# A convolution and a gated network on one core: layer-norm sums on ScalarE for 13 of 16 blocks, x ahead of the weights, and a new order of steps

## The chip, the core and the metric

One core of a Trainium2 chip. The metric is device time in microseconds of one execution, the median of several runs. Names used here: TensorE (PE) multiplies matrices, VectorE (DVE) and ScalarE (ACT) work element by element, GpSimd (POOL) does small side work, SyncE (SP) issues nearly all the DMAs. Each engine runs its own queue of instructions in order; semaphores make one wait for another.

## What is computed

The reference, cut to what matters (S = 2048 tokens, D = 640, F = 1728, all tensors bfloat16):

```python
xn = layernorm(x)                                   # over D, eps 1e-5
# branch A: a short convolution, a long one, a gate
k_shift = sum(k_pad[:, t:t + S, :] * shift_k[:, 3 - t] for t in range(4))
kv = k_shift * v
y = irfft(rfft(kv, 2 * S) * rfft(ssm_k, 2 * S))[:S] + kv * ssm_D
a = xn * y
# branch B: a gated network
h = sigmoid(xn @ w_gate) * (xn @ w_up)
out = x + a + h @ w_down
```

## The kernel before

The 2048 tokens lie as 128 partitions x 16 blocks; one block is a tile of 128 x 640. Four blocks are a group g, and four groups are the four passes t of branch B.

**Norm.** For a block, `ln_stats` (L198) runs two bn_stats over halves of 320 on VectorE, `ln_aggr` (L202) makes mean and variance of them, `ln_var` adds eps, `ln_pow` takes the power -1/2 on GpSimd, and `ln_xn` (L219) writes the normalised block xn on VectorE. In group 0, TensorE transposes a block (`xn_mm`, L233) and ScalarE copies it to xnT (`xn_ev`, L236); the two together are `turn(i)`. In groups 1 to 3 a DMA transposes it (`xn_turn`, L240).

**Branch B.** The 1728 columns are 14 chunks fc of 128, the last one a half chunk. For each chunk `gate_mm` and `up_mm` (L260) make a product of 128 x 512 from five matmuls. `gate_ev` (L269) takes the sigmoid on ScalarE, `up_ev` (L275) multiplies on VectorE and writes hT. `both_mm`, `both_ev` and `both_mul` do the last half chunk. `down_mm` (L304) makes half of a token block's output in two parts of seven matmuls each, and `down_ev` (L309) adds it into x. In pass t = 0 the first two chunks are done token block by token block (`quarter`, L251: five matmuls of 128 x 128), so that they can start when the first block is normalised. gate, up, down and the last products of branch A share four PSUM buffers: a product can start when the fourth product before it has been taken away by its `gate_ev`, `up_ev` or `down_ev`.

**Branch A.** D is five chunks c of 128 channels. `kv_op` (L337 to L346) makes k_shift * v on VectorE: 8 steps for each half of the tokens, the last of which multiplies by v. `h_turn` (L323) transposes the long filter hn on VectorE, `add_D` adds ssm_D on GpSimd. The long convolution is a Fourier transform in two stages: `st1_mm` (L363, L365; eight matmuls a step), `st1_ev` (L223, tile t), a store and a load through HBM (`wr1`, `rd2`), `st2_mm` (L396), `st2_ev`, `prod` on VectorE (L409, L411), and back: `inv1_mm` (L425), `inv1_ev`, `wr2`, `rdb`, `inv2_mm` (L464), and `inv2_q`, `inv2_x`, which gate by xn and add into x. The st1, st2 and inv1 steps share two large PSUM buffers.

**Order.** Start, first group and quarters are written out. All else is put into chains, one letter for each kind of step (g for gate, up and down matmuls, s for gate_ev and both_ev, u for up_ev, both_mul and down_ev, k for kv_op, m for the first loads, and so on), and a string ORDER of 845 letters says from which chain the next step is taken. That string is the order of every engine's queue, SP's too. DMAs go round eight semaphores, so a DMA is issued when the eighth before it has landed.

Of the kernel before, what the change touches and what calls it, by code (L numbers as in the profile page):

```python
# [57 lines left out]
def kernel(  # L58
# [14 lines left out]
    nc = tc.nc  # L73
    xr = A_q.flatten_outer_dims().rearrange("(p b) d -> p b d", b=NB)
# [14 lines left out]
    cv = ctx.enter_context(tc.tile_pool(name="cv", bufs=1))  # L89
    dr = ctx.enter_context(tc.tile_pool(name="dr", bufs=1, space=bass.MemoryType.DRAM))  # L90
# [14 lines left out]
    x = res.tile([P, NB, DM], BF16, name="x")  # L105
    xn = res.tile([P, NB, DM], BF16, name="xn")
# [14 lines left out]
    sync = nc.sync  # L121
# [49 lines left out]
    def load_w(eng, lo, hi, u):  # L171
        if u == 0:
            eng.dma_start(w[:, :, lo:hi], wgr[:, :, lo:hi])  # L173
            return
        h = min(hi, 13 * P)
        eng.dma_start(w[:, :, UP + lo:UP + h], wur[:, :, lo:h])  # L176
# [9 lines left out]

    lns = [dict() for _ in range(4)]

    def ln_stats(g, i):
        b = 4 * g + i  # L190
        d = lns[g]
        if i == 0:
            d["st"] = cv.tile([P, 4, 2, nc.vector.BN_STATS_DIM], F32, name="st")
            d["mv"] = cv.tile([P, 4, nc.vector.BN_AGGR_DIM], F32, name="mv")
            d["var"] = cv.tile([P, 4], F32, name="var")
            d["rstd"] = cv.tile([P, 4], F32, name="rstd")
        for s2 in range(2):
            nc.vector.bn_stats(d["st"][:, i, s2, :], x[:, b, s2 * 320:(s2 + 1) * 320])  # L198

    def ln_aggr(g, i):  # L200
        d = lns[g]
        nc.vector.bn_aggr(d["mv"][:, i, :], d["st"][:, i, :, :])  # L202

    def ln_norms(g, i):
        ln_stats(g, i)
        ln_aggr(g, i)

    def ln_var(g, lo, hi):
        d = lns[g]
        nc.vector.tensor_scalar(d["var"][:, lo:hi], d["mv"][:, lo:hi, 1], 1e-5, None, op0=ALU.add)  # L210

    def ln_pow(g, lo, hi):
        d = lns[g]
        nc.gpsimd.tensor_tensor(d["rstd"][:, lo:hi], d["var"][:, lo:hi], mhalf[:, lo:hi], ALU.pow)

    def ln_xn(g, i):
        b = 4 * g + i
        d = lns[g]
        nc.vector.tensor_scalar(xn[:, b, :], x[:, b, :], d["mv"][:, i, 0:1], d["rstd"][:, i:i + 1],  # L219
                                op0=ALU.subtract, op1=ALU.mult)  # L220
# [9 lines left out]
    def xn_mm(i):  # L230
        xts[i] = pt = psC.tile([P, NC, P], BF16, name="pt", tag="c")
        for c in range(NC):
            nc.tensor.transpose(pt[:, c, :], xn[:, i, c * P:(c + 1) * P], ident[:])  # L233

    def xn_ev(i):
        nc.scalar.copy(out=xnT[:, i, :, :], in_=xts[i][:, :, :])  # L236
# [8 lines left out]
    def quarter(u, fc, i):  # L245

        if i == 0:
            pgs[u, fc] = psG.tile([P, 512], F32, name=("pg", "pu")[u], tag="g")
        o = u * UP + fc * P
        for c in range(NC):  # L250
            nc.tensor.matmul(pgs[u, fc][:, i * P:(i + 1) * P], lhsT=w[:, c, o:o + P], rhs=xnT[:, i, c, :],  # L251
                             start=(c == 0), stop=(c == NC - 1))
# [3 lines left out]
    def product(u, fc):  # L256

        pg = psG.tile([P, 512], F32, name=("pg", "pu")[u], tag="g")
        for c in range(NC):
            nc.tensor.matmul(pg[:, :], lhsT=w[:, c, u * UP + fc * P:u * UP + (fc + 1) * P], rhs=xnT[:, :, c, :],  # L260
                             start=(c == 0), stop=(c == NC - 1))
# [93 lines left out]
    def st1_mm(c, n):  # L355

        h, n4 = divmod(n, 4)
        if n == 0:
            chunks[c]["d1"] = dr.tile([P, 2, NB, 2 * P], BF16, name="d1", bufs=2)
        pss[n] = ps = psC.tile([P, 4, 2 * P], F32, name="ps1", tag="c")  # L360
        for i in range(4):
            b = 4 * n4 + i
            nc.tensor.matmul(ps[:, i, 0:P], lhsT=S1[:, b, h, :], rhs=cin[c]["kvh"][:, 0, b, :], start=True, stop=True)  # L363
            hp = cin[c]["kvh"][:, 1, :, :].rearrange("p b c -> p (b c)").rearrange("p (b c e) -> p b e c", b=8, e=2)
            nc.tensor.matmul(ps[:, i, P:2 * P], lhsT=S1[:, b, h, :], rhs=hp[:, b // 2, b % 2, :], start=True, stop=True)  # L365
# [111 lines left out]
    for b in range(2):  # L477
        for i in range(2):
            (sync, nc.scalar)[i].dma_start(x[:, b, 320 * i:320 * i + 320], xr[:, b, 320 * i:320 * i + 320])
    for u in range(2):  # L480
        load_w((sync, nc.scalar)[u], 0, P, u)
    for i in range(2):
        (sync, nc.scalar)[i].dma_start(x[:, 2 + i, :], xr[:, 2 + i, :])
# [92 lines left out]
    for c in range(NC):  # L576
# [54 lines left out]
    step("o", store, NB - 1, NB, 4 * P, DM)  # L631

    ORDER = """
    mmmmmmmmmggggsmmsumggsguuZsgggmukksmgmskmukgkggkmuksHgsggumkuggskgukHgskgmkmuggmkTsksgKuugkDagaAgkmA
    uaHKtHmwmagllllAglgDPkAuaAwmklllahuelgekAugekakkugaggAgkggkAakaukuewgkukmkkgsTggAkuwsngkVutAgaskwkgs
    AKgaukgrHkaAgAualakswkgAagVguskrAgAbgkwTksuBkBskkguKDgskkHlkaagguAlAKkngbtwushungpkplBsBgaAwgaugkpKl
    gksaupgAAPlglswkVslrgkuKaueaglHAwaggkkAAVDcwCggTkaCkukuaAgregHkkAbggkugBBKkuurpbBgeklgBkgpbpgBluBpeg
    atawAkuWggskuaklpghuAwasgAAgaarluAkHrkggAcVskgkJupgsCbgDswBugkBuspaAaKklgPgpAbugBkFsWrgRkcVCCsgugpdH
    rsbpBkgBugWqudbsgplkpgrBBcurgqRCsqJgbgWkwgukgswpBrBlubksBFqgusludapdqaglgeAaguggRqAeaquAwAappgAaepqe
    ggIcgCuwguJbBgpFdgrbpqugWBuqdpqBrgcugJpqgrCbugpsRwBFggpbupgBdsrqBuWpgdqrcJspggqgCbuFRqBggsubpdsWugBB  # L640
    gdprscCqgpJrqgbsuBgqFRgupsgbspudpgqrWBgBduqqRcpgJCqWgsqbsBugBgpugsRdpgpucsgqJqCWdgqgusqgudgqouggudRq
    gqugoRogggqudguodqgqqdudoggqqqqgogqoouuoooooo
    """
# [35 lines left out]
```

## Time and profile before

| | |
|---|---|
| time, median of 3 runs | 238.88 us (238.79 to 239.32) |
| span of the profiled execution | 236.5 us |
| TensorE busy (PE) | 228.3 us, 97% |
| VectorE busy (DVE) | 205.5 us, 87% |
| ScalarE busy (ACT) | 120.5 us, 51% |
| GpSimd busy (POOL) | 12.7 us, 5% |
| DMA | 56.79 MB, mean 240 GB/s |

The profile is of one execution, and its rows count from its first instruction. For that execution only the span is given: it runs from the first to the last instruction, and the time of a run is 2.4 us longer at the median (238.88 against 236.5). A matmul's end in the profile is modelled, so a row's duration is longer than the step from one matmul to the next; the steps are read from the starts. The granted TensorE clock was 1.000 throughout.

How to read its rows: in the timeline, start and duration in us, engine, line, operation, out<-in, shape, and in brackets how long the engine idled before and what ended that. In the groups: total busy us, mean ns of one, then idle time before them with what ended it. In the waits: who waited for whom, us in total, times, the longest. "SPq" and "ACTq" are the issuing of DMAs.

### The profile page before, as it was taken

How to read it: one execution, taken by the hardware profiler on the slowest of the kernel's cores; microseconds unless marked ns; L12 is line 12 of the kernel's file. 1: busy time of each engine (PE TensorE's matmuls, PEld its weight loads, DVE VectorE, ACT ScalarE, POOL GpSimd, SP SyncE). 2: the span in 40 equal slices, each digit the busy share in tenths (PEclk: the TensorE clock that was granted, in tenths of full speed). 3: DMA queues.
4: the chain of work that ended last, by engine and by line, in shares of the span. 5: the costliest groups of instructions: out<-in, count | busy, mean ns of one | idle time of the engine just before them, and what ended most of it. 6: DMA issues, size and time to landing. Idle time of an engine off the chain costs nothing.

```text
span 236.5 us, 5439 instructions
## 1 busy us (share of the span) xinstructions
PE 228.3 (97%) x2200; PEld 131.2 (55%) x2201; DVE 205.5 (87%) x365; ACT 120.5 (51%) x151; POOL 12.7 (5%) x24
## 2 busy tenths in 40 slices
PE   7799979999999999999999999999999999999994
PEld 2664434877555445766663544487655444446772
DVE  5533879999999999999999999889999979998563
ACT  2342323463376787666767777663346465552000
POOL 5210000020000002000001300000000000000000
PEclk9999999999999999999999999999999999999999
DMA  6999999999999999999889888998799976575774
GB/s 175 272 267 273 238 250 314 247 293 193 232 312 306 285 278 311 250 284 210 230 244 270 215 197 221 308 264 248 180 294 254 240 200 205 148 179 136 201 232 148
DMA packets 98927, 56.79 MB, mean 240 GB/s; under 512 B 58518, under 2 KB 93142, under 8 KB 98646
## 3 DMA queue, kind: packets, MB, share of 16 engines
q1 hardware_dynamic: 97814, 55.95, 91.0%
q10 hardware_dynamic: 1088, 0.49, 0.8%
q8 instruction: 17, 0.28, 0.5%
q14 instruction: 8, 0.07, 0.1%
HBM read 36.12 MB, written 18.35 MB: 230 GB/s over the span
## 4 chain that ended last, share of the span: by engine, by line
PE 68%; DMA 11%; SPq 11%; DVE 5%; ACT 2%; issue 2%; ACTq 0%; DVEq 0%
PE pd L304 20%; PE pu L260 16%; PE pg L260 16%; DMA sraw<-in_A_shift_k_dram 5%; PE psb L464 4%; PE ps L396 3%; PE psa L425 3%; PE ps L363 3%; PE ps L365 3%; DMA hn<-in_A_ssm_k_dram 2%; DMA d<-t 2%; DMA w<-in_B_w_gate_dram 2%; SPq L176 2%; SPq L173 2%; SPq L139 2%
## 5 line engine op out<-in xcount | busy, mean ns | idle before, releaser
L260 PEld LDWEIGHTS <-w 128*128 128x128 bf16 x500 | 46.5, 98 | 56.7 <-issue 7.0
L304 PE MATMUL pd<-wd,hT 128*128 128x320 bf16 (+2 forms) x447 | 65.9, 299 | 0.1
L260 PE MATMUL pu<-xnT,w 128*128 128x512 bf16 x250 | 62.3, 380 | 1.3 <-DVE hT L275 1.3
L260 PE MATMUL pg<-xnT,w 128*128 128x512 bf16 x250 | 62.2, 379 | 0.0
L304 PEld LDWEIGHTS <-hT 128*128 128x128 bf16 x448 | 41.8, 98 | 18.4 <-issue 2.3
L269 ACT ACTIVATE sig<-pg 128x512 bf16<-128x512 f32 x52 | 30.9, 600 | 38.2 <-PE pg L260 31.2
L223 ACT CAST t<-ps 128x1024 bf16<-128x1024 f32 x39 | 38.4, 1014 | 16.7 <-PE ps L365 10.4
L275 DVE TENSOR_TENSOR hT<-sig,pu 128x512 bf16<-128x512 bf16 x52 | 35.2, 679 | 8.9 <-PE pu L260 5.6
L223 ACT CAST xz<-ps 128x1024 bf16<-128x1024 f32 x34 | 33.2, 1015 | 16.1 <-PE ps L396 14.9
L411 DVE TENSOR_TENSOR xz<-xz 128x2048 bf16<-128x2048 bf16 x20 | 24.3, 1217 | 0.1
L363 PE MATMUL ps<-kvh,S1t 128*128 128x128 bf16 x160 | 21.3, 218 | 0.3 <-ACT t L223 0.3
L365 PE MATMUL ps<-kvh,S1t 128*128 128x128 bf16 x160 | 21.3, 220 | 0.0
L341 DVE TENSOR_TENSOR tmp<-kx,sc 128x1024 bf16<-128x1024 bf16 x30 | 20.7, 689 | 0.3
L343 DVE TENSOR_TENSOR acc<-acc,tmp 128x1024 bf16<-128x1024 bf16 x30 | 20.5, 685 | 0.3
L309 DVE TENSOR_TENSOR x<-pd,x 128x320 bf16<-128x320 f32 (+2 forms) x32 | 15.4, 485 | 5.1 <-PE pd L304 4.9
L365 PEld LDWEIGHTS <-S1t 128*128 128x128 bf16 x160 | 15.4, 96 | 2.4 <-issue 0.4
L363 PEld LDWEIGHTS <-S1t 128*128 128x128 bf16 x160 | 15.5, 97 | 2.1
L198 DVE BATCH_NORM_STATS2 st<-x 128x6 f32<-128x320 bf16 x32 | 13.9, 476 | 3.1 <-DMA x<-in_A_q_dram 3.1
L469 DVE TENSOR_TENSOR yx<-psb,xn 128x512 bf16<-128x512 f32 x20 | 13.8, 688 | 2.1 <-PE psb L464 1.7
L409 DVE STREAM_SHUFFLE xz<-xz 128x512 f32<-128x512 f32 x20 | 14.5, 725 | 0.0
L223 ACT CAST ao<-psa 128x1024 bf16<-128x1024 f32 x10 | 9.9, 1013 | 8.4 <-PE psa L425 8.3
L323 DVE STREAM_TRANSPOSE kvh<-hn 128x512 f32<-128x512 f32 x10 | 10.9, 1099 | 1.5 <-DMA hn<-in_A_ssm_k_dram 1.5
(48 smaller groups left out, 150.1 us busy)
## 6 DMA issues: line engine op xcount, KB each, us to landing
d<-t SPq DMA_DIRECT2D x20, 512.0 KB, 5.0
t<-d SPq DMA_DIRECT2D x20, 512.0 KB, 4.7
bi<-d SPq DMA_DIRECT2D x8, 512.0 KB, 5.6
d<-ao SPq DMA_DIRECT2D x6, 512.0 KB, 4.6
kx<-in_A_k_dram SPq DMA_DIRECT2D x10, 256.0 KB, 5.1
hn<-in_A_ssm_k_dram SPq DMA_DIRECT2D x20, 128.0 KB, 4.0
kvh<-in_A_v_dram SPq DMA_DIRECT2D x10, 256.0 KB, 5.3
x<-in_A_q_dram SPq DMA_DIRECT2D x3, 640.0 KB, 5.3
```

The source lines that it names most:

```text
L223: nc.scalar.copy(out=out, in_=in_)
L260: nc.tensor.matmul(pg[:, :], lhsT=w[:, c, u * UP + fc * P:u * UP + (fc + 1) * P], rhs=xnT[:, :, c, :], start=(c == 0), stop=(c == NC - 1))
L269: nc.scalar.activation(sig[fc][:, :], pgs[0, fc][:, :], ACT.Sigmoid)
L275: nc.vector.tensor_tensor(hT[:, fc, :], sig[fc][:, :], pgs[1, fc][:, :], ALU.mult)
L304: nc.tensor.matmul(pd[:, :], lhsT=hT[:, fc, bb * P:(bb + 1) * P], rhs=wd[:, fc, es], start=(fc == 0), stop=(fc == NFC - 1))
L309: nc.vector.tensor_tensor(x[:, 4 * t + bb, es], pds[bb, half][:, :], x[:, 4 * t + bb, es], ALU.add)
L341: nc.vector.tensor_tensor(d["tmp"][:, :, :], kx[:, lo + 3 - m:hi + 3 - m, :], sb(m), ALU.mult)
L343: nc.vector.tensor_tensor(d["acc"][:, :, :], d["acc"][:, :, :], d["tmp"][:, :, :], ALU.add)
L363: nc.tensor.matmul(ps[:, i, 0:P], lhsT=S1[:, b, h, :], rhs=cin[c]["kvh"][:, 0, b, :], start=True, stop=True)
L365: nc.tensor.matmul(ps[:, i, P:2 * P], lhsT=S1[:, b, h, :], rhs=hp[:, b // 2, b % 2, :], start=True, stop=True)
L409: nc.vector.stream_shuffle(z[:, 2, :, :].bitcast(F32), z[:, 1, :, :].bitcast(F32), swap)
L411: nc.vector.tensor_tensor(z[:, 1:3, :, :], z[:, 0:1, :, :].to_broadcast((P, 2, 8, P)), z[:, 1:3, :, :], ALU.mult)
```

## The change

- **Norm sums.** Block 2, and all blocks of groups 1 to 3, no longer use bn_stats. Two passes of ScalarE over the block take their place (`ln_sums`): a Copy scaled by -1/640 whose running sum is minus the mean, and a Square with that as bias whose running sum is the sum of squared differences. Both write their elementwise output into xn, which is overwritten later. Variance and power are made on GpSimd for the groups (`ln_sums_pow`), on VectorE and GpSimd for block 2. VectorE normalises with an add and a multiply (`ln_sums_xn`). Blocks 0, 1 and 3 keep bn_stats.
- **First loads.** x blocks 2 and 3 are asked for before the first gate and up weights, not behind them. ScalarE's queue then issues its halves of x blocks 0 and 1, x block 3 and the first up block.
- **Start.** The first transpose stands ahead of block 3's statistics; the other three `turn`s are put between the quarters by the list FIRST.
- **HBM tiles.** d1 and d2 get a buffer for each chunk in place of two.
- **Order.** ORDER is a new string of 842 letters, and TURNS permutes the chain of the first loads (m) and that of the stores (o). In the first loads, the up weights of chunks 4 and 5 and of 8 and 9 now come ahead of the gate weights of 4 and 5; x group 1 is asked for seventh from there on, both halves of w_down late, and v's first half of chunk 1 last but for one table. VectorE evicts 19 of the large PSUM tiles, not 15.

The diff, cut:

```diff
+FIRST = """
+g00 t1 u00 t2 g10 u10 t3 g01 u01 g11 u11 g02 u02 g12 u12 g03 u03 g13 u13
+"""
...
+    def ln_sums(g, i):
+        b = 4 * g + i
+        d = ln_tile(g)
+        nc.scalar.activation(xn[:, b, :], x[:, b, :], ACT.Copy, scale=-1.0 / DM, accum_out=d["nm"][:, i:i + 1])
+        nc.scalar.activation(xn[:, b, :], x[:, b, :], ACT.Square, bias=d["nm"][:, i:i + 1],
+                             accum_out=d["ss"][:, i:i + 1])
+
+    def ln_sums_var(g, i):
+        d = lns[g]
+        nc.vector.tensor_scalar(d["var"][:, i:i + 1], d["ss"][:, i:i + 1], 1.0 / DM, 1e-5, op0=ALU.mult, op1=ALU.add)
+
+    def ln_sums_pow(g, lo, hi):
+        d = lns[g]
+        nc.gpsimd.tensor_scalar(d["var"][:, lo:hi], d["ss"][:, lo:hi], 1.0 / DM, 1e-5, op0=ALU.mult, op1=ALU.add)
+        ln_pow(g, lo, hi)
+
+    def ln_sums_xn(g, i):
+        b = 4 * g + i
+        d = lns[g]
+        nc.vector.tensor_scalar(xn[:, b, :], x[:, b, :], d["nm"][:, i:i + 1], d["rstd"][:, i:i + 1],
+                                op0=ALU.add, op1=ALU.mult)
...
-            chunks[c]["d1"] = dr.tile([P, 2, NB, 2 * P], BF16, name="d1", bufs=2)
+            chunks[c]["d1"] = dr.tile([P, 2, NB, 2 * P], BF16, name="d1", bufs=NC)
...
+    for i in range(2):
+        (sync, nc.scalar)[i].dma_start(x[:, 2 + i, :], xr[:, 2 + i, :])
     for u in range(2):
         load_w((sync, nc.scalar)[u], 0, P, u)
-    for i in range(2):
-        (sync, nc.scalar)[i].dma_start(x[:, 2 + i, :], xr[:, 2 + i, :])
...
     busy(10)
-    for i in range(4):
-        ln_stats(0, i)
-        if i:
-            ln_xn(0, i - 1)
-        ln_aggr(0, i)
-        ln_var(0, i, i + 1)
-        ln_pow(0, i, i + 1)
+    ln_stats(0, 0)
+    ln_ready(0, 0)
+    ln_sums(0, 2)
+    ln_stats(0, 1)
+    ln_xn(0, 0)
+    ln_ready(0, 1)
+    turn(0)
+    ln_stats(0, 3)
+    ln_sums_var(0, 2)
+    ln_pow(0, 2, 3)
+    ln_xn(0, 1)
+    ln_ready(0, 3)
+    ln_sums_xn(0, 2)
     ln_xn(0, 3)
-    turn(0)
     busy(3)
-    for i in range(4):
-        for k in range(4):
-            quarter(k % 2, k // 2, i)
-            if k == (0, 1, 1, 3)[i] and i < 3:
-                turn(i + 1)
+    for k in FIRST.split():
+        if k[0] == "t":
+            turn(int(k[1]))
+        else:
+            quarter("gu".index(k[0]), int(k[1]), int(k[2]))
...
-            step("l", ln_norms, g, i)
-        step("l", ln_var, g, 0, 4)
-        step("P", ln_pow, g, 0, 4)
+            step("L", ln_sums, g, i)
+        step("P", ln_sums_pow, g, 0, 4)
...
-    mmmmmmmmmggggsmmsumggsguuZsgggmukksmgmskmukgkggkmuksHgsggumkuggskgukHgskgmkmuggmkTsksgKuugkDagaAgkmA
...
+    mmgmmgsummggggsmsugmmgmgLsuuLsZgLkkggskkmggmmuusggnkLsmuLugsPmkmgumgHgggsLusguggllsuggguHggummgggkmL
...
+    TURNS = {"m": [1, 7, 4, 9, 21, 0, 20, 2, 10, 5, 6, 13, 12, 14, 8, 17, 15, 11, 22, 18, 16, 19, 23, 25, 24, 3],
+        "o": [2, 0, 4, 1, 5, 3, 7, 6, 8, 11, 10, 9, 12, 13]}
+    left = {k: iter([v[i] for i in TURNS.get(k, range(len(v)))]) for k, v in chains.items()}
```

More of the change, by code (lines that the diff above doesn't have):

```diff
@@ L187, with ln_tile @@
     lns = [dict() for _ in range(4)]
+    def ln_tile(g):
+        if "q" not in lns[g]:
+            q = cv.tile([P, 4, 4], F32, name="lnq", bufs=2)
+            lns[g] = dict(q=q, nm=q[:, 0, :], ss=q[:, 1, :], var=q[:, 2, :], rstd=q[:, 3, :])
+        return lns[g]
     def ln_stats(g, i):
         b = 4 * g + i
-        d = lns[g]
+        d = ln_tile(g)
         if i == 0:
@@ L194, in ln_stats @@
             d["mv"] = cv.tile([P, 4, nc.vector.BN_AGGR_DIM], F32, name="mv")
-            d["var"] = cv.tile([P, 4], F32, name="var")
-            d["rstd"] = cv.tile([P, 4], F32, name="rstd")
         for s2 in range(2):
@@ L202, in ln_aggr @@
         nc.vector.bn_aggr(d["mv"][:, i, :], d["st"][:, i, :, :])
-    def ln_norms(g, i):
-        ln_stats(g, i)
-        ln_aggr(g, i)
+    def ln_sums(g, i):
+        b = 4 * g + i
+        d = ln_tile(g)
+        nc.scalar.activation(xn[:, b, :], x[:, b, :], ACT.Copy, scale=-1.0 / DM, accum_out=d["nm"][:, i:i + 1])
[13 more added lines that the diff above has]
+                                op0=ALU.add, op1=ALU.mult)
     def ln_var(g, lo, hi):
@@ L418, in inv1_mm @@
         if y2 == 0:
-            d["d2"] = dr.tile([32, P, P], BF16, name="d2", bufs=2)
+            d["d2"] = dr.tile([32, P, P], BF16, name="d2", bufs=NC)
         d["pa", y] = ps = [psC.tile([P, 2, 512], F32, name="psa", tag="c") for _ in range(2)]
@@ L498, in turn, with ln_ready @@
         xn_ev(i)
+    def ln_ready(g, i):
+        ln_aggr(g, i)
+        ln_var(g, i, i + 1)
+        ln_pow(g, i, i + 1)
     busy(10)
-    for i in range(4):
-        ln_stats(0, i)
-        if i:
-            ln_xn(0, i - 1)
-        ln_aggr(0, i)
-        ln_var(0, i, i + 1)
-        ln_pow(0, i, i + 1)
+    ln_stats(0, 0)
[11 more added lines that the diff above has]
+    ln_sums_xn(0, 2)
     ln_xn(0, 3)
-    turn(0)
     busy(3)
-    for i in range(4):
-        for k in range(4):
-            quarter(k % 2, k // 2, i)
-            if k == (0, 1, 1, 3)[i] and i < 3:
-                turn(i + 1)
+    for k in FIRST.split():
[3 more added lines that the diff above has]
+            quarter("gu".index(k[0]), int(k[1]), int(k[2]))
     for fc in range(2):
@@ L519 @@
         up_ev(0, fc)
-    chains = {k: [] for k in "ABCDHKPRTVWZabcdeghklmnopqrstuw"}
+    chains = {k: [] for k in "ABCDHKLPRTVWZabcdeghklmnopqrstuw"}
     def step(k, fn, *args):
@@ L615 @@
         for i in range(4):
-            step("l", ln_norms, g, i)
-        step("l", ln_var, g, 0, 4)
-        step("P", ln_pow, g, 0, 4)
+            step("L", ln_sums, g, i)
+        step("P", ln_sums_pow, g, 0, 4)
         for i in range(4):
-            step("l", ln_xn, g, i)
+            step("l", ln_sums_xn, g, i)
         for i in range(4):
@@ L633 @@
     ORDER = """
-    mmmmmmmmmggggsmmsumggsguuZsgggmukksmgmskmukgkggkmuksHgsggumkuggskgukHgskgmkmuggmkTsksgKuugkDagaAgkmA
[L635 to L642, printed above, removed]
-    """
-    left = {k: iter(v) for k, v in chains.items()}
+    mmgmmgsummggggsmsugmmgmgLsuuLsZgLkkggskkmggmmuusggnkLsmuLugsPmkmgumgHgggsLusguggllsuggguHggummgggkmL
+    mLlmDkaaTkkkluAgkkkueAeekggggktkkekkuaaHgukAmAgsawAakgAPgsuuHlmkuKgmkkkTagskkKwwauAAggDkkgKaashtukkk
+    AkAggkgwmwsuslauaAAHgklgkkuVVskaaAAggaksgkkkwAaAggrbuugkkkwsuBBgpkKrHpDasATaAtkugsKnguwwbKBgKFgasgAa
+    AggasuskkpkkVkahwAnrLAwLgguugkpHHgaaAkAgggDcukCJLggeealuALuaIwggbrkeBBgggeurkkkVTuukkKkubggBBgbBgBpw
+    rgppkasupaAIuggstkkkukVwkWaAaAhskgugPaAarkpggAcksJCggbwsuuHHKggDBWlpgBrassupukakggpAAsbBBgggkucwkRss
+    VkkCJggbBupupdqggrrqBspWsbupgguBdBcskrJCgqgbggkFRBusubgFllpBwgaAudaggaAWdarrqqgpAAlgwpppeauqRagAIuqq
+    egeecJCuuggubFpBpWpggbrrggBBuudqdcCJwwgqpgsRWgqpbFBpggsuurbBBprpggssugucdJCWdgpbsgqFBgubBBpqsgpgspuc
+    rCgJgspqqubgugqRdBBdrbWpqqgpgsugqqBBpcCJprsuggbsuBBRdqWpgsdRRpgggsqqucuJCgggWsqduqqdqggudquqdRRooggg
+    gqoggoooqqududugqqqguqooddqqqqgggougoouooo
+    """
+    TURNS = {"m": [1, 7, 4, 9, 21, 0, 20, 2, 10, 5, 6, 13, 12, 14, 8, 17, 15, 11, 22, 18, 16, 19, 23, 25, 24, 3],
+        "o": [2, 0, 4, 1, 5, 3, 7, 6, 8, 11, 10, 9, 12, 13]}
+    left = {k: iter([v[i] for i in TURNS.get(k, range(len(v)))]) for k, v in chains.items()}
     for k in "".join(ORDER.split()):
```

## The prediction

> **What bounds the kernel now.** I read the page first, then a table of windows, then TensorE's timeline where it is not full.
>
> ```profile
> span 236.5 us, 5439 instructions
> ...
> PE 228.3 (97%) x2200; PEld 131.2 (55%) x2201; DVE 205.5 (87%) x365; ACT 120.5 (51%) x151; POOL 12.7 (5%) x24
> ...
> GB/s 175 272 267 273 238 250 314 247 293 193 232 312 306 285 278 311 250 284 210 230 244 270 215 197 221 308 264 248 180 294 254 240 200 205 148 179 136 201 232 148
> ```
> ```profile
> 45.00:135.00 90.00, 89.75 (x837) 54.24 (x835) 88.48 (x167) 59.89 (x74) 6.91 (x7) 1.00 1.02 261
> ```
>
> The columns of a window are its length, then PE, weight loads, DVE, ACT and POOL busy. From 45 to 135 us TensorE is busy for 89.75 of 90 us and VectorE for 88.48; ScalarE has a third of that stretch free. TensorE sets the end: it does the same matrix work in both kernels, so a change of order can win only what TensorE waits, and can lose as much as it is made to wait anew. VectorE is just in time for it. What TensorE waits for lies mostly before 35 us:
>
> ```profile
> 8.64 0.44 PE L251 MATMUL pu<-xnT,w 128*128 128x128 bf16 x5
> 8.92 0.44 PE L251 MATMUL pg<-xnT,w 128*128 128x128 bf16 x5
> ...
> 11.36 0.44 PE L251 MATMUL pg<-xnT,w 128*128 128x128 bf16 x5 [0.22 <-ACT xnT L236]
> ...
> 14.26 1.02 PE L260 MATMUL pg<-xnT,w 128*128 128x512 bf16 x4
> ```
> ```profile
> 31.52 1.24 PE L260 MATMUL pg<-xnT,w 128*128 128x512 bf16 x5
> 32.30 1.10 DVE L323 STREAM_TRANSPOSE kvh<-hn 128x512 f32<-128x512 f32 x1 [1.54 <-DMA hn<-in_A_ssm_k_dram]
> ...
> 34.02 1.24 PE L260 MATMUL pu<-xnT,w 128*128 128x512 bf16 x5 [1.25 <-DVE hT L275]
> ```
> ```profile
> 73.81 0.06 PE ps L365
> 73.87 1.08 PE pg L260 x5
> ...
> 226.20 0.95 PE pd L304 x7
> ...
> 233.28 0.29 DVE x L309
> ```
> ```profile
> PE ps L363 <- ACT t L223: 0.3, 1, 0.3
> ```
>
> A product of five matmuls takes 1.08 us, seven down matmuls 0.95, an st1 step of eight matmuls 0.45 (8 x 0.056). But from 31.52 to 34.02 one took 2.50: VectorE stood at h_turn, which waited for hn, with the up_ev that frees TensorE's buffer queued behind it. That is 1.4 us lost. The eviction of t costs 0.3 us more. After that I find no wait of TensorE to the end.
>
> **The change, part by part.**
>
> *Start.* The quarters (0.28 us each, 8.64 to 8.92) end at 14.26, with holes where a transpose or its copy is late. The new list puts the transposes t1 to t3 between the first quarters, and blocks 2 and 3 of x are asked for before any weight. What it cannot move is the last of the first weights:
>
> ```profile
> 3.17 0.52 SPq L176 DMA_DIRECT2D w<-in_B_w_up_dram  x1
> 3.20 0.38 ACTq L483 DMA_DIRECT2D x<-in_A_q_dram  x1
> ```
> ```profile
> w<-in_B_w_up_dram SPq DMA_DIRECT2D x1, 160.0 KB, 5.7
> x<-in_A_q_dram ACTq DMA_DIRECT2D x1, 160.0 KB, 5.0
> ```
>
> The second up block lands at 3.17 + 5.7 = 8.87, the last x block at 3.20 + 5.0 = 8.20. The bytes asked for up to that up block are the same set in both kernels, so I keep 8.87 for it. In the new list u10 needs it; behind it stand t3 and twelve quarters: 8.87 + 14 x 0.28 = 12.8, the lower bound for the first full product (14.26 now). The upper bound: the first up block is now issued by ScalarE in the place of the last x block (3.20), and if it comes no earlier than 8.87, then u00, t2 and g10 (0.84) also stand behind it, and with another 0.2 for a copy that is late (the 0.22 at 11.36) it is 13.9. I take 13.05, nearer the lower end, since the row for that place in the queue gives 8.20. Gain 1.2 (0.4 to 1.5). Block 2's sums on ScalarE stand ahead of the copy of xnT block 0; what that takes (half a us or more) is covered by the wait for the weights.
>
> *The h_turn stall.* Now the v and k loads and hn are asked for in another order, and the first h_turn stands behind the up_ev of product 10, not 7. Its hn is 7.5 MB into the loads, as before (32.3), while VectorE comes to it at 13.05 + 19.44 + 0.9 = 33.4 (18 products of 1.08 at its up product's end). The 1.4 us go, with 1.1 us to spare.
>
> *A clock for the loads.* A slice of the GB/s row is 5.91 us, so by 29.6 us the DMA engines had moved 7.24 MB and by 32.3, when hn landed, 7.9 MB: a load lands some 1.5 us after the engines have moved as much as was asked for up to and with it. By that, the gate block for product 4 (3.47 MB in the new order) lands at 16.4 and is wanted at 13.05 + 4 x 1.08 = 17.4; block group 1 of x (4.13 MB) lands at 18.9, wanted by ScalarE after gate_ev 4 at 13.05 + 5.4 + 0.85 = 19.3.
>
> *The sums.* Of the 13 blocks 12 leave VectorE in the steady stage:
>
> ```profile
> L198 DVE BATCH_NORM_STATS2 st<-x 128x6 f32<-128x320 bf16 x32 | 13.9, 476 | 3.1 <-DMA x<-in_A_q_dram 3.1
> L202 DVE BATCH_NORM_AGGREGATE mv<-st 128x2 f32<-128x12 f32 x16 | 3.3, 208 | 0.4
> L236 ACT COPY xnT<-pt 128x640 bf16<-128x640 bf16 x4 | 2.8, 692 | 7.7 <-PE pt L233 7.7
> L269 ACT ACTIVATE sig<-pg 128x512 bf16<-128x512 f32 x52 | 30.9, 600 | 38.2 <-PE pg L260 31.2 <-DVE hT L275 5.3 <-PE pg L251 0.5
> L223 ACT CAST t<-ps 128x1024 bf16<-128x1024 f32 x39 | 38.4, 1014 | 16.7 <-PE ps L365 10.4 <-DMA d<-t 5.7 <-ACT ao L223 0.5
> ```
>
> VectorE loses 12 x (2 x 0.476 + 0.208) = 13.9 us, and takes back four evictions of some 1.2 us that the new order sends to it (19 for 15). ScalarE gains 13 x 2 passes over 640 elements. No row has a pass with a running sum; between the 512-wide 0.600 and the 1024-wide 1.014, and nearest to the 0.692 copy of 640, I take 0.72 each, so 18.7 us on an engine with 116 us free. Bounds 15.6 and 26.4: neither fills it. Behind a pair of passes (1.45) stand the gate_ev of the next product; a gate_ev has 3.24 us (three products) until its buffer is wanted and takes 0.6, so one pair ahead of it is hidden, even at 2.03; it isn't where the pair also waits for x. For block group 1 of x there is 0.4 us before that begins (18.9 against 19.3), and some 2 us more before TensorE feels it.
>
> The Trainium skill, "ScalarE: Activation LUTs", Rules for kernel authors, speaks against this move: add and multiply belong on VectorE, which is faster per element. The rows agree (1.16 against 1.45 a block), but the time goes to an engine with room. By the page's figures under "What ACT_TABLE_LOAD costs" a pair would be 1.53 us, an estimate; the sum stays.
>
> *VectorE's chain.* This is where the new order is tightest. It idles longer before 40 us, since kv_op's second half waits for loads moved back. From the first down_ev (behind 23 products and three down parts: 27.7 us after the first product) up to the up_ev that up product 8 of t=1 needs, it has, by the new order, 37 kv_op, 8 down_ev, 7 up_ev, 5 normalisations and 4 h_turn. Back to back they cost:
>
> ```profile
> 34.57 0.60 DVE hT L275
> ...
> 36.36 0.60 DVE tmp L341
> 36.97 1.03 DVE kvh L323
> ...
> 55.77 0.70 DVE acc L343
> ```
>
> 37 x 0.65 + 7 x 0.60 + 4 x 1.03 + 8 x 0.40 + 5 x 0.36 = 37.4 us (0.40 and 0.36 are estimates, from the 0.60 of an up_ev by their smaller tiles), against 17 x 1.08 + 13 x 0.95 + 16 x 0.45 = 37.9 of TensorE's work in between. It has no slack there: each late input in that stretch is a wait of TensorE, one for one. Behind it VectorE runs ahead, by the 13.9 us. I allow 1.0 us of new waits there and at the t buffers (0 to 2.5), and put against it the 0.3 of the old t wait, whose surroundings are rearranged.
>
> *The rest.* d1 and d2 with a buffer per chunk remove waits of writes for old reads, which TensorE doesn't show: nothing. All shapes keep their times; the tail (last down matmul, down_ev at 233.28, one store) is the same work in the same order: some 3 us to the span's end.
>
> **Sum.** The span was 236.5 and the median 238.88: 2.4 us lie around the span, and I keep them. 238.88 - 1.2 - 1.4 - 0.3 + 1.0 = 237.0.
>
> **The rivals.**
> 1. *No new wait.* The chain's 0.5 us hold and the loads come on time: 238.88 - 2.9 = 236.0, or 235.7 with the start at its lower bound. For it: VectorE's 88.48 of 90 us shows that so close a fit held for long.
> 2. *Slower: one load pins the chain.* kv_op 7 of chunk 1 multiplies by the first half of v, which the new order asks for last of its chunk, behind four transposes, a store of t and a halo in SP's queue:
>
> ```profile
> 53.08 5.64 SPq L240 DMA_TRANSPOSE xnT<-xn  x4
> ```
> ```profile
> kvh<-in_A_v_dram SPq DMA_DIRECT2D x10, 256.0 KB, 5.3
> ```
>
> VectorE wants it after 17 kv_op, 8 down_ev, 3 h_turn, 3 normalisations and an up_ev of the chain (19.0 us): 13.05 + 27.9 + 19.0 = 60.0. By the clock of the loads (14.5 MB) it lands at 58.7. By SP's queue it can be later: the last transpose waits for a normalisation that VectorE ends 5.8 us into the chain, at 46.8; with 5.6 us of transposes and some five issues of 0.5 us behind that, v is asked for at 55 and lands at 60.3. From 60.0 on every us is TensorE's. Slower than before needs it past 62.9; landing at 64.5 gives 236.0 + 4.5 = 240.5. For it: two estimates of the landing stand on both sides of the need. Against: it must be 4 us later than the later one.
> 3. *The order hides nothing:* the waits that go come back as waits of the same size (t buffers; the gate block for product 4, 1 us ahead of its need): 2.9 us of them give 238.9.
>
> **How the numbers follow.** The forecast has 0.56, the first rival 0.16, the third 0.08, the second 0.20. About 0.2% (0.5 us) is what a measurement of this kernel can tell from no change. So faster 0.72, same 0.08, slower 0.20. The forecast's bounds are 237.0 - 0.3 - 1.0 = 235.7 and 237.0 + 0.8 + 1.5 = 239.3; the range, 235.5 to 239.3, also holds the first and the third rival, and leaves out the second.
>
> **What the profile after would show.** First full product at 13.05 (12.8 to 13.9); no gap before an up product near 33; sums of 0.65 to 0.85 us a pass and ScalarE at 58 to 60%; VectorE's busy time down by 8 to 10 us; a wait of TensorE for VectorE, if any, between 54 and 80 us. Wrong would be: a first product later than 14; TensorE waiting over 2 us between 45 and 85; a ScalarE pass over 1.1 us; a wait for weights of product 4.

## The result, and the profile after

| | before | after |
|---|---|---|
| time, median | 238.83 us (4 runs, 238.68 to 239.32) | 236.32 us (4 runs, 235.69 to 237.14) |
| profiled execution: time, span | not given, 236.5 us | 236.47 us, 234.5 us |

The ratio is 0.9901 (95% interval 0.9875 to 0.9927), a gain of 2.5 us. The forecast was 237.0 (235.5 to 239.3), with 0.72 for faster. The total is right; the runs below show that one of its three gains is not there, and that another brings nothing by itself. The ratios, here and below, leave out executions that are over 1.5% above the fastest of their kernel; the medians keep them.

The page of after, for the engines:

```profile
span 234.5 us, 5457 instructions
...
PE 227.0 (97%) x2201; PEld 130.8 (56%) x2201; DVE 198.5 (85%) x327; ACT 136.3 (58%) x199; POOL 12.1 (5%) x27
```

VectorE lost 7.0 us and ScalarE gained 15.8. The windows of after, cut at its first full product (columns: length, then PE, weight loads, DVE, ACT and POOL busy, granted clock, DMA share, GB/s):

```profile
0.00:13.87 13.87, 10.27 (x113) 7.18 (x114) 5.57 (x19) 6.44 (x12) 4.80 (x15) 1.00 0.97 226
13.87:45.00 31.13, 31.13 (x165) 15.78 (x163) 18.19 (x29) 20.23 (x45) 3.47 (x6) 1.00 1.05 284
45.00:135.00 90.00, 89.95 (x825) 54.18 (x824) 86.47 (x138) 63.40 (x87) 3.87 (x6) 1.00 0.94 250
135.00:210.00 75.00, 74.43 (x889) 38.89 (x888) 72.19 (x115) 44.41 (x55) 0.00 (x0) 1.00 0.88 231
```

From 13.87 to 135 TensorE is idle for 0.05 us: the wait at 32 is gone, and so is the one for the eviction of t. What remains stands in the waits of TensorE and in its timeline at 192 (the first three waits lie ahead of the first full product; `idle` is the tile of the multiplies whose result is not used):

```profile
PE pg L279 <- ACT xnT L264: 1.7, 1, 1.7
PE idle L522 <- DVE hT L120: 1.2, 1, 1.2
PE pt L261 <- DVE xn L247: 0.7, 1, 0.7
PE psa L453 <- DVE xz L437: 0.6, 1, 0.6
```
```profile
13.87 1.24 PE L288 MATMUL pg<-xnT,w 128*128 128x512 bf16 x5
...
191.99 0.65 PE L453 MATMUL psa<-xz,SMt 32*32 32x512 bf16 x32 [0.57 <-DVE xz L437]
```

A useful split is at the first full product. From there to the start of the last matmul there are 218.77 us in the trace of before (14.26 to 233.03) and 217.13 in that of after (13.87 to 231.00). So of the 2.0 us between the two spans 1.64 come from the steady stage and 0.39 from the start; some 3.5 us from the last matmul to the span's end are the same in both. The other 0.5 us of the measured gain lie between one profiled execution and the medians.

The steady stage repeats: the profiled execution of every later run of the new order without an edit in that stage, on three chips, took 217.12 to 217.19 us. The start does not repeat, as the experiments show.

### The profile page after: what moved, and what is told of

It is laid out like the page before. It is cut to its first block, busy times and chain, and to the rows that moved or that the text cites. A ratio compares the mean times of both kernels' runs of the same rounds, so it can differ in the third digit from the quotient of the medians.

```text
span 234.5 us, 5457 instructions
## 1 busy us (share of the span) xinstructions
PE 227.0 (97%) x2201; PEld 130.8 (56%) x2201; DVE 198.5 (85%) x327; ACT 136.3 (58%) x199; POOL 12.1 (5%) x27
## 5 line engine op out<-in xcount | busy, mean ns | idle before, releaser
L332 PE MATMUL pd<-wd,hT 128*128 128x320 bf16 (+2 forms) x448 | 64.5, 299 | 0.0
L303 DVE TENSOR_TENSOR hT<-sig,pu 128x512 bf16<-128x512 bf16 x52 | 34.7, 680 | 15.2 <-PE pu L288 11.1
L251 ACT CAST t<-ps 128x1024 bf16<-128x1024 f32 x37 | 36.0, 1013 | 18.7 <-PE ps L393 16.0
L393 PE MATMUL ps<-kvh,S1t 128*128 128x128 bf16 x160 | 20.8, 219 | 0.0
L391 PE MATMUL ps<-kvh,S1t 128*128 128x128 bf16 x160 | 20.8, 218 | 0.0
L337 DVE TENSOR_TENSOR x<-pd,x 128x320 bf16<-128x320 f32 (+2 forms) x32 | 14.9, 481 | 5.3 <-PE pd L332 5.2
L251 ACT CAST ao<-psa 128x1024 bf16<-128x1024 f32 x8 | 8.1, 1012 | 8.9 <-PE psa L453 8.8
L215 ACT ACTIVATE xn<-x 128x640 bf16<-128x640 bf16 x13 | 9.5, 732 | 3.5 <-DMA x<-in_A_q_dram 3.5
L254 DVE CAST ao<-psa 128x1024 bf16<-128x1024 f32 x8 | 9.8, 1222 | 2.0 <-PE psa L453 1.9
```

The costliest lines, as they stand in the source:

```text
L251: nc.scalar.copy(out=out, in_=in_)
L303: nc.vector.tensor_tensor(hT[:, fc, :], sig[fc][:, :], pgs[1, fc][:, :], ALU.mult)
L332: nc.tensor.matmul(pd[:, :], lhsT=hT[:, fc, bb * P:(bb + 1) * P], rhs=wd[:, fc, es], start=(fc == 0), stop=(fc == NFC - 1))
L337: nc.vector.tensor_tensor(x[:, 4 * t + bb, es], pds[bb, half][:, :], x[:, 4 * t + bb, es], ALU.add)
```

## The experiments

A run is compared with runs of before on the same chip. "Steady" is the trace's time from the first full product to the start of the last matmul.

| run | median us | before, us | ratio (95%) | first full product | steady |
|---|---|---|---|---|---|
| old start, new order | 236.72 | 238.10 | 0.9938 (0.9912 to 0.9965) | 13.26 | 217.12 |
| new start, old order | 238.08 | 238.10 | 1.0010 (0.9985 to 1.0036) | 15.26 | 218.72 |
| sums alone | 251.46 | 238.10 | 1.0580 (1.0547 to 1.0613) | 13.65 | 232.55 |
| h_turn later alone | 239.15 | 238.10 | 1.0027 (0.9997 to 1.0057) | 13.24 | 220.67 |
| after again | 236.18 | 237.57 | 0.9962 (0.9936 to 0.9988) | 13.57 | 217.13 |
| bn_stats, new order | 240.02 | 237.57 | 1.0104 (1.0078 to 1.0130) | 15.27 | 221.23 |
| VectorE + 3 us | 239.29 | 237.57 | 1.0075 (1.0052 to 1.0098) | 13.51 | 220.47 |
| start, both edits | 236.00 | 237.57 | 0.9932 (0.9906 to 0.9959) | 13.18 | 217.19 |
| block 2 on VectorE | 236.50 | 238.37 | 0.9929 (0.9900 to 0.9959) | 13.64 | 217.12 |
| new list alone | 237.08 | 238.37 | 0.9953 (0.9926 to 0.9981) | 13.96 | 217.12 |
| two buffers | 236.18 | 238.37 | 0.9919 (0.9889 to 0.9949) | 13.39 | 217.13 |
| both edits and the swap | 235.51 | 238.37 | 0.9897 (0.9865 to 0.9929) | 13.02 | 216.50 |

Each has one profiled execution, so the last two columns are of one execution each, and those of "new start, old order" and "bn_stats, new order" are of executions in which TensorE's clock fell at the start (run 2). Before spread from 236.2 to 240.5 us in 66 executions, after from 235.7 to 238.2 in 16.

**1. The new order with the old start.** The loads, the statistics of block 2 and the quarters of before, all else as in after:

```diff
+    for u in range(2):
+        load_w((sync, nc.scalar)[u], 0, P, u)
     for i in range(2):
         (sync, nc.scalar)[i].dma_start(x[:, 2 + i, :], xr[:, 2 + i, :])
-    for u in range(2):
-        load_w((sync, nc.scalar)[u], 0, P, u)
...
-    ln_sums(0, 2)
...
-    for k in FIRST.split():
+    for i in range(4):
+        for k in range(4):
+            quarter(k % 2, k // 2, i)
```

> The changed kernel with the start of before (weights ahead of x blocks 2 and 3, bn_stats for block 2, the old order of the quarters) and the new order of all later steps. Theory A: the later steps bring most of the gain, since the first full product came only 0.39 us earlier with the new start (13.87 against 14.26): 236.3 + 0.4 = 236.7 us (236.4 to 237.0), first full product at 14.2 to 14.3, no wait near 33 us. Rival B, the sizes of the prediction: the start is worth 1.2 us, so 237.5 us.

236.72 us, as theory A has it; but the first full product came at 13.26, a microsecond before the 14.26 of before with the same start. The profiled execution of before had a late load. VectorE's statistics of block 2, in before and in run 4, which has the same start:

```profile
7.06 0.89 DVE L198 BATCH_NORM_STATS2 st<-x 128x6 f32<-128x320 bf16 x2 [1.24 <-DMA x<-in_A_q_dram]
```
```profile
6.01 0.89 DVE L198 BATCH_NORM_STATS2 st<-x 128x6 f32<-128x320 bf16 x2
```

The bracket is the tell: 1.24 us idle for x in the one, none in the other, and the statistics come 1.05 us later. The 14.26 that the prediction started from was one execution's bad luck with a load.

**2. The new start with the old order.** The reverse edit.

> The kernel before with the start of the changed one alone. Theory A: the first full product comes at 13.87, 0.39 us earlier, but the h_turn in the old order still waits for hn, which lands by the bytes ahead of it at 32.3 as before, so the end moves by 0 to 0.4 us: 238.5 to 238.85 us, and the wait of TensorE near 32 us grows. Rival B, the sizes of the prediction added up: 1.2 us, 237.6 us.

No gain, as theory A says, though not by its way: TensorE has no wait near 32 in this trace, but one of 1.27 us at 72.5. The trace, of an execution of 239.26 us, shows something else. Windows of this run, from the gap ahead of the first quarter on (the eighth column is the granted clock):

```profile
5.00:8.38 3.38, 1.42 (x10) 0.58 (x9) 2.31 (x9) 2.33 (x5) 1.01 (x3) 0.99 1.26 254
8.38:11.90 3.52, 3.52 (x36) 3.52 (x36) 1.08 (x4) 1.38 (x2) 0.85 (x2) 0.53 1.18 288
11.90:15.26 3.36, 3.36 (x64) 3.36 (x62) 0.02 (x1) 1.34 (x3) 0.63 (x1) 1.00 1.03 260
```
```profile
8.38 0.69 PE L284 MATMUL pg<-xnT,w 128*128 128x128 bf16 x5 [1.66 <-ACT xnT L269]
8.87 0.74 PE L266 MATMUL pt<-ident,xn 128*128 128x128 bf16 x5
```

TensorE stood for 1.66 us, since ScalarE's pair of passes on block 2 is ahead of the copy of xnT block 0, and over the next 3.5 us its granted clock was 0.53 in the mean: a quarter took 0.53 us in place of 0.28, and the first full product came at 15.26. Of 59 runs of kernels with that pair in the first group, 8 had a mean clock of 0.984 to 0.993; in after again (run 5) the two such executions took 238.0 and 238.2 us, the other ten 235.8 to 236.8. Of 111 runs of kernels without it, before among them, none was below 0.997. Run 3 is left out of that count: its waits are longer, and all six of its executions are at 0.985 to 0.993.

**3. The sums alone.** In the order of before, ScalarE's sums in the places of bn_stats:

```diff
-            step("l", ln_norms, g, i)
-        step("l", ln_var, g, 0, 4)
-        step("P", ln_pow, g, 0, 4)
+            step("l", ln_sums, g, i)
+        step("P", ln_sums_pow, g, 0, 4)
         for i in range(4):
-            step("l", ln_xn, g, i)
+            step("l", ln_sums_xn, g, i)
```

> The kernel before, order and start unchanged, with the norm sums of groups 1 to 3 on ScalarE in the places where bn_stats stood. Theory A: TensorE did not wait for VectorE in the steady stage of before, so 13.9 us taken from VectorE bring nothing by themselves: 238.5 to 239.2 us, VectorE busy down by 13 us. Rival B: the closely filled VectorE costs TensorE time that its records do not show as waits; then a gain of over 1 us, below 237.8. Rival C: ScalarE's pair of passes stands where gate_ev or t evictions are wanted, or where x is late: over 239.5 us with new waits of TensorE for ScalarE.

Rival C, and far beyond its size: 13.4 us slower. ScalarE's timeline and TensorE's:

```profile
46.47 0.74 ACT L216 ACTIVATE xn<-x 128x640 bf16<-128x640 bf16 x1
47.11 0.20 ACT L216 ACTIVATION_READ_ACCUMULATOR xn<-x 128x1 f32 x1
47.34 0.83 ACT L217 ACTIVATE xn<-x,lnq 128x640 bf16<-128x640 bf16 x1
48.08 0.19 ACT L217 ACTIVATION_READ_ACCUMULATOR xn<-x,lnq 128x1 f32 x1
...
53.19 1.90 ACT L255 CAST t<-ps 128x1024 bf16<-128x1024 f32 x2
```
```profile
54.23 0.22 PE L395 MATMUL ps<-kvh,S1t 128*128 128x128 bf16 x1 [4.55 <-ACT t L255]
```

The old order has a group's four blocks in a row, because on VectorE that did no harm. On ScalarE they are 6.7 us (46.47 to 53.19) ahead of the evictions of t, and TensorE waits for 4.55 us of them; later groups do the same in smaller pieces, 10.7 us of waits for ScalarE in all behind the first full product. Behind the 4.55 us the granted clock is 0.50 from 54.50 to 57.80; that costs another 1.7 us, an estimate from half of these 3.3 us. So not all of the 13.4 us is the price of the sums' place. ScalarE has room, but not for four pairs in a row. After has them one by one, mostly 2.2 to 4.4 us apart (19.96, 22.12, 24.28, 28.59, and so on), and once two in a row (39.51 and 41.19).

**4. The first h_turn later.** One letter of the order of before moved behind two up_ev:

```diff
-...kukmuksHgsggumkuggskgukHgskg...
+...kukmuksgsggumkuggskgukHHgskg...
```

> The kernel before with one step moved: the first h_turn stands just ahead of the second one in the order, so two up_ev that free TensorE's buffers are no longer queued behind its wait for hn. Theory A: the 1.4 us of TensorE's wait at 31.5 to 34.0 go: 237.4 us (237.1 to 237.7), no product over 1.3 us long near 33. Rival B: VectorE, busy for 88.48 of 90 us from 45 to 135, has no slack to catch up, and the wait comes back behind it: 238.5 to 238.9 us.

Rival B: no gain, and whether the 239.15 us, a little over its range, are a loss the interval does not tell. The wait near 32 is gone and the steady stage is 1.9 us longer. The waits of TensorE in this run:

```profile
PE pg L260 <- DMA xnT<-xn: 1.0, 1, 1.0
PE ps L363 <- ACT t L223: 0.6, 1, 0.6
PE pd L304 <- issue: 0.5, 1, 0.5
```

In starts of matmuls these are 1.2 us at 59 for the first product of the next pass, 0.8 at 73 (0.4 in before) and 0.9 at 41 for a down matmul whose hT VectorE wrote late. VectorE had not gained what TensorE had: with h_turn moved it stands at the next step that needs a load, the multiply by v.

```profile
32.06 0.69 DVE L346 TENSOR_TENSOR kvh<-acc,kvh 128x1024 bf16<-128x1024 bf16 x1 [1.93 <-DMA kvh<-in_A_v_dram]
```

The largest wait is no late input of VectorE, which had normalised the first block of group 1 by 51.8 and the last by 53.3: the group's transposes stand in SP's queue behind the next chunk's hn loads. In this run, and in after:

```profile
50.41 2.98 SPq L139 DMA_DIRECT2D hn<-in_A_ssm_k_dram  x4
53.51 5.26 SPq L240 DMA_TRANSPOSE xnT<-xn  x4
```
```profile
45.62 5.27 SPq L268 DMA_TRANSPOSE xnT<-xn  x4
```

From the first full product that is 40.3 us here, 38.8 in before (53.08) and 31.8 in after. This run started a microsecond sooner than the trace of before and had a stall less, and the transposes were asked for no earlier. The first product of the next pass, in before and here:

```profile
60.24 1.24 PE L260 MATMUL pg<-xnT,w 128*128 128x512 bf16 x5
```
```profile
60.26 1.24 PE L260 MATMUL pg<-xnT,w 128*128 128x512 bf16 x5 [1.04 <-DMA xnT<-xn]
```

In before it has no wait; here TensorE is ready a microsecond sooner and waits for the transposes until the same moment. In run 2 the product starts at 59.99. So in three traces of the old order it comes within 0.3 us, whether the first full product came at 13.24, 14.26 or 15.26: the transposes, behind the loads in SP's queue, take back both the earlier start and the missing stall. Of the 1.9 us by which the steady stage is longer, 1.0 is thus only this run's earlier start. In after the last transpose landed at 54.04 and that product started at 55.72: 1.7 us to spare.

**5. After, again**, beside the next three.

> The changed kernel itself beside the others of this set. Theory A (the change is worth 2.5 us wherever it runs): 0.9901 of before. Theory B (part of it is the start, which differs from run to run with the arrival of the first loads and the granted clock): the same kernels scatter by about 1 us, the ratio is 0.990 to 0.996, and the kernel with the old start (236.72 us, 0.9938) is level with it.

Theory B. On this chip before is faster (237.57) and after the same (236.18). The old start with the new order is level with it by the ratio (0.9938). By the medians the change is worth 1.4 us here and 2.5 us in the first set; its copy with two buffers (run 11) has 2.2 us on a third chip.

**6. bn_stats on VectorE in the new order.**

```diff
-            step("L", ln_sums, g, i)
-        step("P", ln_sums_pow, g, 0, 4)
+            step("L", ln_norms, g, i)
+        step("P", ln_norms_pow, g, 0, 4)
         for i in range(4):
-            step("l", ln_sums_xn, g, i)
+            step("l", ln_xn, g, i)
```

> The changed kernel, its order unchanged, with bn_stats on VectorE again for the blocks of groups 1 to 3, each in the place where ScalarE's sums stand (block 2 of the first group stays on ScalarE). VectorE gets 12 x 1.16 = 13.9 us back, 9.3 of it between 20 and 42 us and 4.6 between 95 and 107. Theory A (VectorE is just in time, as its 37.4 us of work against 37.9 of TensorE's says): it enters that stretch late and TensorE waits, 1 to 4 us more than the changed kernel. Rival B: the 12.9 us that VectorE idles between 13.87 and 45.00 take the first eight blocks, and the last four are made up: no more than 0.5 us.

Theory A: 3.8 us more than after in the median, 4.1 in the steady stage. The windows show where:

```profile
15.27:45.00 29.73, 29.73 (x155) 14.81 (x153) 22.36 (x46) 7.67 (x13) 2.45 (x3) 1.00 1.04 282
45.00:135.00 90.00, 87.07 (x799) 52.19 (x797) 88.02 (x152) 52.55 (x65) 3.84 (x5) 1.00 0.92 235
135.00:210.00 75.00, 74.43 (x876) 39.08 (x874) 72.82 (x116) 45.97 (x57) 0.42 (x1) 1.00 0.91 239
```

VectorE still idles for 7 us before 45, yet TensorE loses 2.9 us between 45 and 135. So the sums on ScalarE are worth about 4 us in the new order and cost 13 in the old one. And the gain needs both: the new order without the sums of groups 1 to 3 is 1.0% slower than before, these sums without the new order 5.8%.

**7. Three microseconds more for VectorE.**

```diff
         else:
+            if c == 1 and lo == 0:
+                for _ in range(5):
+                    nc.vector.tensor_tensor(d["tmp"][:, :, :], d["acc"][:, :, :], d["acc"][:, :, :], ALU.mult)
             kv = d["kvh"][:, 0, lo:hi, :]
```

> The changed kernel with five more multiplies of 128x1024 on VectorE (0.6 us each, 3.0 us together; their result is not used) just ahead of the step that multiplies by the first half of v for chunk 1, at 61.05 us. Theory A (no slack in VectorE's chain): the end moves by 3.0 us less the lead that VectorE has over TensorE near 80 us, 1 to 2 us: 1 to 2 us more, TensorE waiting for VectorE between 62 and 100. Rival B: all 3.0 us come through. Rival C: VectorE makes it up and nothing comes through.

```profile
60.69 3.59 DVE L375 TENSOR_TENSOR tmp<-acc 128x1024 bf16<-128x1024 bf16 x5
64.20 0.68 DVE L377 TENSOR_TENSOR kvh<-acc,kvh 128x1024 bf16<-128x1024 bf16 x1
```
```profile
68.31 1.24 PE L288 MATMUL pg<-xnT,w 128*128 128x512 bf16 x5 [1.46 <-DVE hT L303]
```

Rival B. The five took 3.51 us (60.69 to 64.20) and the steady stage grew by 3.34. VectorE's lead was 0.2 us, not 1 to 2: the first one to wait is a product at 68, for an up_ev, not one near 80.

**8. Another start.** Block 2 by bn_stats on VectorE, and the list "g00 t1 g10 g01 t2 g11 u10 u11 u00 t3 u01 g02 g12 u12 u02 g03 u03 g13 u13".

> The changed kernel with another start: block 2 normalised by bn_stats on VectorE like blocks 0, 1 and 3, so that ScalarE's first work is the copy of xnT block 0; and the quarters listed so that those of the last weights to land come late: g00 t1 g10 g01 t2 g11 u10 u11 u00 t3 u01, then the rest. Theory A (the pair on block 2 and the order of the first quarters kept the start at 13.87): first full product at 12.6 to 12.8, and the end follows by as much, 1.1 us less than the changed kernel of the same set. Rival B: a later load or VectorE's chain pins the steady stage, and the end moves by under 0.4 us. Rival C: TensorE's gap of 1.7 us before the first quarter also made its granted clock fall in some runs; without the gap the scatter of the times shrinks.

First full product at 13.18, not 12.6 to 12.8: one quarter waited 0.49 us for the copy of xnT block 1. The steady stage is the same (217.19), so no later load took the earlier start back. But the median is only 0.2 us below that of after again, not 1.1: theory A's size was not reached, and the number is rival B's, though what rival B gave as the reason is not seen. TensorE idles for 0.3 us ahead of the first quarter, the clock is 0.999 or more in all 7 runs, and they lie within 235.5 to 236.4, where after again has 235.8 to 238.2. That is as rival C has it, though 7 runs alone would not show it; the count under run 2 does.

**9 and 10. Each edit by itself.** First only block 2 on VectorE, then only the list.

> The changed kernel with one thing undone: block 2 by bn_stats on VectorE, so that ScalarE's pair no longer stands ahead of the copy of xnT block 0; the list of the quarters stays. Theory A (two things hold the start, and either alone suffices): the first quarter comes at 7.0 with the first gate weights, but in the list 17 steps of 0.28 us stand from the first up quarter on, whose weights land at 8.7 to 9.1: first full product at 13.5 to 13.8, against 13.57 of the changed kernel, and the end within 0.3 us of it (236.0 to 236.4). Rival B (ScalarE's pair alone held it): 13.0 or less, 235.6 us. In both TensorE's gap ahead of the first quarter is under 1 us, and if that gap made the granted clock fall in some runs, none shows a mean clock under 0.995.

> The changed kernel with the new list of the quarters alone (g00 t1 g10 g01 t2 g11 u10 u11 u00 t3 u01, then the rest); block 2 stays on ScalarE. Theory A (either thing alone suffices to hold the start): the first quarter waits for the copy of xnT block 0 behind ScalarE's pair, to 8.2 to 8.5, and 19 steps of 0.28 us follow: 13.5 to 13.8, the end as the changed kernel's (236.0 to 236.4), and some runs at a mean clock of 0.993 that are 2 us longer. Rival B (only the order of the weights held it): 13.0, 235.6 us.

The first full products came at 13.64 and 13.96, as against 13.18 with both edits: as theory A has it, either thing holds the start, though the second came later than its 13.5 to 13.8. The times missed: 236.50 and 237.08 us, where both were to be 236.0 to 236.4. In the first the first up quarter waits for its weights (0.83 us, to 8.41), and no run is below 0.998. In the second the first quarter waits for ScalarE until 7.98, and a quarter behind it for another 0.5 us; two of its 12 runs are at a clock of 0.984 and 0.993, 239.8 and 238.55 us.

**11. Two buffers for d1 and d2**, as before: `bufs=NC` becomes `bufs=2` twice.

> The changed kernel with d1 and d2 in two buffers each as before. Theory A (writes that wait for old reads are off TensorE's path): no difference, 236.0 to 236.4 us, 217.1 us from the first full product to the last matmul. Rival B (in the new order a write of t waits for the reads of two chunks before, holds SP's queue and with it the loads): over 0.5 us more.

Nothing: steady 217.13, 236.18 us.

**12. Both edits at the start and a swap.** Against the kernel of run 8:

```diff
-g00 t1 g10 g01 t2 g11 u10 u11 u00 t3 u01 g02 g12 u12 u02 g03 u03 g13 u13
+t1 g00 g10 g01 g11 u10 t2 u11 u00 u01 t3 g02 u02 g12 u12 g03 u03 g13 u13
...
-    ln_stats(0, 2)
+    ln_half(0, 2, 0)
     ln_xn(0, 1)
+    ln_half(0, 2, 1)
...
-...gFBgubBBpqsgpgspuc
+...gFBgubBBpqsgpgsucp
```

> The kernel with both edits at the start, and two more. The list begins t1 g00 g10 g01 g11 u10 t2 u11 u00 u01 t3, and block 1 is normalised between the two halves of block 2's statistics, 0.4 us sooner. And one shuffle of VectorE (prod of group 16), for which TensorE waited 0.6 to 0.7 us near 191 although the matmuls there do not use what it writes, is put behind those matmuls, with the up_ev that followed it ahead of them. Expected by the sums: first full product at 12.7 to 12.9 (13.18 with the two edits alone), 216.5 to 216.7 us from there to the last matmul (217.13), so 235.0 to 235.2 us against 236.0 with the two edits alone. Rival: the earlier start meets a load (the gate weights for product 4, wanted 1 us after they land) and gives its part back, 235.4 us; or the shuffle behind the matmuls delays VectorE's chain and the 0.6 us come back later: 235.6 us.

```profile
13.02:45.00 31.98, 31.98 (x171) 16.35 (x169) 19.00 (x31) 20.22 (x45) 3.47 (x6) 1.00 1.07 286
45.00:135.00 90.00, 89.95 (x837) 53.86 (x836) 86.36 (x138) 63.65 (x87) 3.88 (x6) 1.00 0.95 250
135.00:210.00 75.00, 75.00 (x907) 39.04 (x906) 72.59 (x116) 44.39 (x55) 0.00 (x0) 1.00 0.91 233
```
```profile
190.51 0.65 PE L453 MATMUL psa<-xz,SMt 32*32 32x512 bf16 x32
```
```profile
191.49 0.72 DVE L437 STREAM_SHUFFLE xz<-xz 128x512 f32<-128x512 f32 x1
```

235.51 us, the fastest of all: 0.67 less than after's order on the same chip (the run with two buffers), 0.9897 of before. The swap gave all it promised: the steady stage is 216.50, and VectorE shuffles while TensorE is already in the next product. The start gave less than summed (13.02, not 12.7 to 12.9: TensorE had two waits of 0.2 us that the sum had not), and the time missed its 235.0 to 235.2 by 0.3 us.

## Why the prediction was right, and where it was not

**The start: mis-sized.** The step was 14.26 to 13.05, a gain of 1.2 (0.4 to 1.5). The two profiled executions give 0.39, its lower bound; but over executions at full clock the old start gives 14.26, 13.65, 13.26 and 13.24, and the new one 13.87, 13.57, 13.51 and 13.39: means of 13.60 and 13.59. With four traces each that spread over 1.0 and 0.5 us, the gain is nil as far as they can tell, below the range that was given; runs 1 and 2 agree, and 8 of the 59 executions with the new pair at the start lost time by the clock besides. Two things failed. The 14.26 was taken as the kernel's start, though its row showed a wait for a load that other executions don't have. And that the time of block 2's sums ahead of the copy is "covered by the wait for the weights" was wrong: x block 2 landed at 6.10, the pair ran to 7.81, and the first quarter came at 8.53 with its weights in place since 6.9; the first up block landed at 8.94, which is the condition that the upper bound of 13.9 named. Runs 9 and 10 speak for both holding it, with one trace each.

**The h_turn stall: right in size, not by itself.** The 1.4 us at 32 are gone. Hn landed at 31.28 and VectorE came to it at 34.17 (32.3 and 33.4 in the working). But run 4 has the same stall removed in the old order, and nothing comes of it: by the first product of the next pass TensorE is where it was in before. The term was counted as if it stood alone, and behind it stood another load and the transposes. The new order also asks for the transposes some 7 us sooner; that this is what lets the 1.4 us through fits the traces, but no run moved the transposes alone.

**The t wait, 0.3:** gone. **New waits, 1.0:** one, of 0.6 us, and at 192, not between 54 and 80. It is not a late input: VectorE's shuffle wrote a third of xz that the matmuls skip, and yet they waited for it; run 12 takes it away by order alone. Together these three terms were -0.7 in the working and -1.64 in the traces; the start was -1.2 there and -0.4 here. The errors nearly cancel, which is why the total fits to 0.7 us: that part is luck.

**The sums.** A pass was to take 0.72:

```profile
L215 ACT ACTIVATE xn<-x 128x640 bf16<-128x640 bf16 x13 | 9.5, 732 | 3.5 <-DMA x<-in_A_q_dram 3.5
L216 ACT ACTIVATE xn<-x,lnq 128x640 bf16<-128x640 bf16 x13 | 10.8, 828 | 0.4
L215 ACT ACTIVATION_READ_ACCUMULATOR xn<-x 128x1 f32 x13 | 2.5, 191 | 0.0
L216 ACT ACTIVATION_READ_ACCUMULATOR xn<-x,lnq 128x1 f32 x13 | 2.4, 186 | 0.0
```

0.73 and 0.83, and behind each an instruction of 0.19 us that reads the running sum, which the working did not have. A pair is 1.70 us from start to start (46.47 to 48.17 in run 3), not 1.45; the 1.53 that the prediction estimated from the Trainium skill, "ScalarE: Activation LUTs", "What ACT_TABLE_LOAD costs", is nearer and still 0.17 us short. ScalarE is at 58% as forecast. That one pair ahead of a gate_ev is hidden holds in after; run 3 shows what four are. VectorE's busy time fell by 7.0 us, not by the 8 to 10 that were forecast: its rows for statistics lose 14.0 us and the four evictions bring back some 5, as in the working, but the rows overlap and don't add up to the busy time.

**VectorE's chain: right.** "It has no slack there": 3.34 of 3.51 us came through in run 7. In run 6, 4.1 of 13.9 us came through; VectorE's idle time before 45 us (12.9 us in after, 7.4 there) took up part of the rest. That "the time goes to an engine with room" is worth some 4 us there, more than any single term of the sum; the sum had it only as the reason why nothing got worse.

**Rival 2, the late v, did not come:** its kv_op ran at 61.05, v had landed at 58.88 (60.0 and 58.7 in the working). The margin was 2.2 us, and run 7 shows what the price past it would have been. A later v itself was not tried. The gate weights for product 4 landed at 17.16, 1.0 us ahead of their need, and d1 and d2 are worth nothing, both as said.

**Open:** how much of the gain each piece of the new order brings by itself. In the old order the first product of the second pass hangs on SP's queue of loads, as run 4 shows, and that would fit its larger scatter (medians from 237.6 to 238.8 in four sets of runs, where after and its copy with two buffers have 236.2 to 236.3); but no run varied the order of the loads alone.

## What to carry to other kernels

Move work to an idle engine only in pieces that fit between what that engine is waited for: the same sums cost 13 us four in a row and gained 4 spread out, in an order made for them. In an order as tight as this one a wait that is removed alone is handed on, so price it by what is just in time behind it, an engine or a queue of loads. And read a start stage from several executions: a bracket that names a DMA can be a sign that the row is of that execution, not of the kernel.

## What the runs showed of the hardware

TensorE's granted clock fell to half after an idle gap of only 1.66 us (run 2) or 1.58 us (run 6), for 3.4 us. By their mean clock it did so in 8 of 59 executions of kernels that have this gap; the gap of 1.7 us in the trace of after passed at full clock. The Trainium skill, "TensorE: Matmul & The Clock Gate", Part 1, agrees with the length and the chance of it: the clock follows activity over free-running windows of about 3.4 us, by which the outcome would depend on how the gap falls into a window. The traces fit that as far as they go. Cut into pieces of 3.41 us from the moment at which the record of the clock begins (4.87 in run 2, 4.97 in run 6), these two have a piece in which TensorE is busy for 1.5 us, and the clock is 0.50 in the next one; in the five traces that have the gap at full clock the emptiest piece has 1.7 to 2.5 us. The Trainium skill's rule under "Why this matters for your kernels", no idle gaps over some 3 us, is too mild by these runs: half of that was enough, with TensorE busy for 1.42 of the 3.38 us before the first quarter.
